# Delta-rule attention and routed experts: keys and queries times the states of two heads in one block-diagonal product, the masked product on four array positions, ranks in two products

## The chip, the cores and the metric

The kernel runs on one core of a Trainium2 chip. The metric is the device time of one execution in microseconds (us). A core has a matrix engine (PE, with its weight loads listed as PEld), a vector engine (DVE), a scalar engine (ACT), GpSimd (POOL) and a queue engine (SP). [...] Each engine runs its own instructions in order and waits for semaphores of the others.

## The reference

Attention with a delta rule on 4 x 8 heads, 768 steps, head dimension 48, and a top-1 mixture of 8 experts on the 3072 resulting rows of 384:

```python
for t in range(S):
    kt, vt, bt = (k_n[:, :, t], v[:, :, t], beta[:, :, t, None])
    y[:, :, t] = np.einsum('bhd,bhde->bhe', q[:, :, t], state)
    v_old = np.einsum('bhde,bhd->bhe', state, kt)
    state = state + bt[:, :, :, None] * np.einsum('bhd,bhe->bhde', kt, vt - v_old)
...
logits = x @ w_gate
expert_idx = np.argmax(logits, axis=1)
...
for e in range(E):
    lo, hi = (boundaries[e], boundaries[e + 1])
    h = np.maximum(x_sorted[lo:hi] @ w1[e], 0.0)
    y_sorted[lo:hi] = h @ w2[e]
return (gate_w[:, None] * y).astype(np.float32)
```

k_n is k over its norm, x the attention output with the heads side by side, gate_w the softmax weight of the chosen expert.

## The kernel before

All data are float32. The 768 steps are cut into 12 chunks t of 64 steps. The 32 heads are numbered by f (8), e (2) and x (2): e picks the half of the 128 partitions in which the 48 features of a head stand (partitions 64e to 64e+47), x the half in which its 64 steps stand. `products()` runs over the 32 heads. A float32 product is two passes, a pass being one weight load and one matmul, so a group of 32 products is 64 passes.

For each chunk, `scores(t)` (L311) multiplies keys with keys and queries; every two chunks `invert(n)` inverts triangular 32 x 32 blocks on DVE, with some 170 short instructions; `turn(t)` is the recurrence: `values` (L495) puts v into the PSUM banks BR, `with_state` (L480) adds keys times the state, ACT copies the sum to R, `inverse` (L512), `across` (L522) and `inverse` again give Z, with an ACT copy behind each, and `kz` (L536) adds keys times Z to the state in the banks BS, which ACT copies to S for the next chunk. `output(t)` is `with_state` again for the queries (into the banks BY) and `masked` (L557), 32 products of the masked scores with Z; ACT copies the rows x and SP writes them to `xs` in DRAM. Bank BR+e holds all heads of one e.

`logits(t)` transposes the rows (L578) and multiplies them with the gate (L586). `route(m, part)` works on groups of four tiles of 128 rows (five groups, then two groups of two): part 0 finds the expert on DVE (one-hot `oh`), part 1 ranks the rows within their experts by `ranks` on PE (L632, L638: for four tiles 8 products, 16 passes) and POOL writes (row, gate) entries into two lists in DRAM (L669, one indirect DMA per tile).

Expert 0 takes its first 256 rows early: `early_rows` loads their entries (`both_e`), a minimum of the two lists gives `rows_e` (L865), and POOL gathers the rows. `entries` loads the rest after the last route (`both_l`, three DMAs on SP and three on ACT; `rows`, L763). `turned_rows` (L797), `hidden` (L815) and `second` (L844, L897 for the last 32 rows) are the experts; `weights(e)` loads 3 MB on SP in five DMAs.

The order on each engine is not the order of the code. A planner (class `Plan`) takes every operation with its estimated cost, passes and priority, plays it forward and emits all engines in the order of the starts that it finds; `passes` feeds a model of the matrix engine's instruction pages (PAGE 128 passes, FILL 3.8).

## Time and profile before

| | |
|---|---|
| three runs | 646.66, 647.83, 650.55 us, median 647.83 |
| the profiled execution | 645.72 us, span 644.0 us, mean granted clock 0.875 |
| busy | PE 84%, PEld 58%, DVE 35%, ACT 23%, POOL 16% |
| 0 to 57 us | loads, first scores, first inversion |
| 57 to 310 us | chunks 0 to 11 and routing |
| 310 to 644 us | early rows of expert 0, then the experts |

The span counts from the first to the last instruction; 1.7 us of the execution lie around it. The granted clock is a share of TensorE's full speed; it has two levels, so a mean of 0.75 says that half of the stretch ran at each. A busy PE may still be waiting inside a group of passes.

### The profile page before, as it was taken

The page shows a single profiled execution, that of the slowest core. Times are in us where ns is not written, and L with a number is a line of the kernel's source. Part 1 is how long each engine was busy: PE and PEld are TensorE (multiplying, and loading weights), DVE is VectorE, ACT ScalarE, POOL GpSimd, SP SyncE. Part 2 cuts the span into 40 slices and gives each one's busy share as a digit, 9 for nine tenths or more (in the row PEclk, how much of TensorE's full clock was granted, in tenths as well). Part 3 has the DMA queues.
Part 4 walks back from the last instruction along what each step waited for, and adds up shares of the span by engine and source line. Part 5 has one row for each costly group of instructions (what it writes and reads, how often), then busy time and mean ns, then how long its engine had stood idle before and what let it go on. Part 6 is the DMA issues. An engine that isn't in the chain of part 4 may idle for free. (4 is left out here: it accounts for less than half of the span.)

```text
span 644.0 us, 17055 instructions
## 1 busy us (share of the span) xinstructions
PE 540.8 (84%) x7496; PEld 374.6 (58%) x7497; DVE 226.1 (35%) x921; ACT 151.2 (23%) x297; POOL 101.8 (16%) x109
## 2 busy tenths in 40 slices
PE   4448878989889978947696799999999999999990
PEld 4236667977777857746454555555555555555550
DVE  2976998885775680002100111201111101210100
ACT  2453445245244322321000110111101010110100
POOL 2000000320201002020206030402213040201011
PEclk9999879688588756755697899999999999999996
DMA  8964424433123225207403523433422340100000
GB/s 197 241 136 133 135 79 122 137 98 114 52 63 100 77 94 183 92 3 246 133 3 96 182 78 110 154 100 128 145 85 88 107 160 1 39 1 24 14 12 24
DMA packets 29933, 64.16 MB, mean 100 GB/s; under 512 B 6006, under 2 KB 18214, under 8 KB 29856
## 3 DMA queue, kind: packets, MB, share of 16 engines
q1 hardware_dynamic: 24240, 52.47, 27.0%
q0 software_dynamic: 4352, 9.47, 4.7%
q10 hardware_dynamic: 1264, 1.10, 0.8%
q8 instruction: 59, 0.97, 0.7%
q14 instruction: 18, 0.15, 0.1%
HBM read 49.62 MB, written 11.04 MB: 94 GB/s over the span
## 5 line engine op out<-in xcount | busy, mean ns | idle before, releaser
L815 PE MATMUL pair<-kqA,blkA 128*128 128x416 f32 (+2 forms) x288 | 91.7, 477 | 5.8 <-ACT kqA L824 4.3
L844 PE MATMUL pair<-blkA,kqA 128*128 128x384 f32 x240 | 80.0, 491 | 0.0
L815 PEld LDWEIGHTS pair<-kqA,blkA 128*128 128x128 f32 x288 | 55.2, 205 | 39.8 <-issue 28.6
L821 DVE TENSOR_SCALAR kqA<-pair 128x416 f32<-128x416 f32 (+2 forms) x36 | 19.5, 543 | 144.9 <-PE pair L815 83.1
L844 PEld LDWEIGHTS pair<-blkA,kqA 128*128 128x128 f32 x240 | 45.0, 190 | 34.7 <-issue 5.6
L744 POOL DMA_INDIRECT out<-y,rows_i x30 | 28.9, 963 | 224.3 <-ACT y L835 157.5
L311 PE MATMUL pair<-kqA 48*64 48x128 f32 (+1 forms) x896 | 38.7, 329 | 26.2 <-ACT pA L256 15.4
L815 PE MATMUL pair<-kqA,pA 128*128 128x416 f32 x144 | 51.1, 514 | 0.3 <-ACT y L835 0.3
L512 PE MATMUL pair<-R,blkA 32*32 32x48 f32 x1536 | 36.2, 253 | 17.4 <-issue 9.4
L311 PEld LDWEIGHTS pair<-kqA 48*64 48x64 f32 x896 | 31.3, 184 | 31.5 <-ACT pA L256 17.8
L844 PE MATMUL pair<-pA,kqA 128*128 128x384 f32 x144 | 48.1, 491 | 0.0
L824 ACT ACTIVATE kqA<-pair 128x416 f32<-128x416 f32 (+2 forms) x36 | 17.2, 478 | 131.2 <-PE pair L815 93.3
L669 POOL DMA_INDIRECT lists<-ent,ri x24 | 27.9, 1162 | 108.7 <-DVE ri L657 57.6
L512 PEld LDWEIGHTS pair<-R,blkA 32*32 32x32 f32 x1536 | 30.5, 154 | 22.9 <-issue 12.5
L832 DVE TENSOR_SCALAR y<-pair,rows 32x384 f32<-32x384 f32 (+1 forms) x15 | 8.5, 607 | 92.8 <-ACT y L835 85.4
L815 PEld LDWEIGHTS pair<-kqA,pA 128*128 128x128 f32 x144 | 27.1, 190 | 22.7 <-issue 21.1
L844 PEld LDWEIGHTS pair<-pA,kqA 128*128 128x128 f32 x144 | 26.9, 190 | 21.2 <-issue 3.7
L480 PE MATMUL pair<-S,kqA 48*64 48x48 f32 x1408 | 34.5, 250 | 3.0 <-issue 2.9
L835 ACT ACTIVATE y<-pair,rows 128x384 f32<-128x384 f32 x15 | 8.7, 580 | 113.9 <-PE pair L844 108.3
L737 POOL DMA_INDIRECT kqA<-xs,rows_i x30 | 29.8, 994 | 27.3 <-DVE rows_i L734 18.4
L480 PEld LDWEIGHTS pair<-S,kqA 48*64 48x64 f32 x1408 | 30.4, 163 | 5.7 <-issue 5.1
L557 PE MATMUL pair<-Z,pA 64*64 64x48 f32 x768 | 33.5, 258 | 0.0
(113 smaller groups left out, 677.9 us busy)
## 6 DMA issues: line engine op xcount, KB each, us to landing
kqA<-in_kq SPq DMA_DIRECT2D x46, 192.0 KB, 4.4
blkA<-in_w SPq DMA_DIRECT2D x15, 512.0 KB, 4.3
blkA<-in_w SPq DMA_DIRECT2D x10, 768.0 KB, 5.2
v<-in_vtok SPq DMA_DIRECT2D x12, 384.0 KB, 3.6
kt<-in_ktok SPq DMA_DIRECT2D x12, 384.0 KB, 6.1
xs<-x SPq DMA_DIRECT2D x24, 192.0 KB, 2.1
pA<-in_w SPq DMA_DIRECT2D x9, 512.0 KB, 4.7
pA<-in_w SPq DMA_DIRECT2D x6, 768.0 KB
```

The lines of the kernel that those rows point to most:

```text
L311: nc.tensor.matmul(bk[bank + e][half(x), i * w : i * w + w].rearrange("p (k c) -> p k c", c=C), lhsT=v[feat(e), 0, x * FQ + f, :], rhs=v[f ...
L480: nc.tensor.matmul(sh(bank + e)[half(x), f, :], lhsT=KQ(t)[feat(e), k, x * FQ + f, :], rhs=Sbs[t % 2][feat(e), x, f, :], start=first and f ...
L512: nc.tensor.matmul(sh(BZ + e)[quad(q), f, :], lhsT=tt[quad(q), :, 16 * u + 8 * e + f], rhs=R[quad(q), e, f, :], start=True, stop=True, ski ...
L557: nc.tensor.matmul(sh(BY + e)[half(x), f, :], lhsT=Pm(t)[half(x), e, f, :], rhs=Zbs[t % 2][half(x), e, f, :], start=(t == 0 and f == 0), s ...
L669: P.op("POOL", 1.0, lambda i=i: nc.gpsimd.indirect_dma_start(out=lists[i % 2], out_offset=bass.IndirectOffsetOnAxis(ap=ri[:, i : i + 1], a ...
L737: nc.gpsimd.indirect_dma_start(out=dst, out_offset=None, in_=xs, in_offset=bass.IndirectOffsetOnAxis(ap=idx, axis=0), bounds_check=N - 1, ...
L744: nc.gpsimd.indirect_dma_start(out=out, out_offset=bass.IndirectOffsetOnAxis(ap=idx, axis=0), in_=src, in_offset=None, bounds_check=N - 1, ...
L815: nc.tensor.matmul(bk[b][:, 0:n], lhsT=a1[:, s, f * 128 : f * 128 + 128], rhs=xT[:, s, :], start=(s == 0), stop=(s == NK - 1))
L821: (lambda f=f, b=b: nc.vector.tensor_scalar(out=hT[:, f, :], in0=bk[b][:, 0:n], scalar1=0.0, scalar2=None, op0=OP.max))
L824: (lambda f=f, b=b: nc.scalar.activation(out=hT[:, f, :], in_=bk[b][:, 0:n], func=AF.Relu)),
L835: (lambda: nc.scalar.activation(out=y[0:n], in_=bk[b][0:n, 0:DM], func=AF.Copy, scale=gate)),
L844: nc.tensor.matmul(bk[b][:, 0:DM], lhsT=hT[:, f, at : at + 128], rhs=a2[:, f, :], start=(f == 0), stop=(f == NF - 1))
```

## The change

- `with_state`: the states of two heads (e = 0 and 1) stand as diagonal blocks of a 128 x 96 tile, so that one product with 112 partitions and 96 columns serves both: 16 products (32 passes) in place of 32 (64 passes). The keys and queries need zeros in the partitions between the heads: POOL clears ring slots, one is cleared by DMA, and the state tiles are cleared once.
- BR, BZ and BY now hold bank by f // 4, with e inside; R, Z and v follow. Each masked product and each query product of f >= 4 writes the other half of the partitions, which the host turns back.
- The copy of the state is two: the half of the partitions with e = 0 on ACT, that with e = 1 on DVE.
- `ranks`: two products (4 passes) on all tiles at once; their second operand `up` is a running sum that DVE makes (a copy and n - 1 additions).
- `both_e` is loaded from POOL's queue, `both_l` from SP's alone, and the weights of experts 1 and 2 wait for `rows`.
- Costs and passes of the planner follow, and the order of all engines with them.

```diff
+    P.op("DVE", 1.0, lambda: nc.vector.memset(pairs[1][:], 0.0), w=kb(BR), prio=-49)
+    for i in range(2):
+        P.op("POOL", 1.4, lambda i=i: nc.gpsimd.memset(Sbs[i][:], 0.0), w=[("S", i, e) for e in range(2)], prio=-15)
+    for i in (2, 3, 4, 5):
+        P.op("POOL", 1.85, lambda i=i: nc.gpsimd.memset(kqA[:, 2048 * i : 2048 * i + 2048], 0.0),
+             w=kKQ(i) + [("zero", i)], prio=-60)
+    for e in range(2):
+        r = slice(64 * e + D, 64 * e + 64)
+        P.op("SP", 0.6, dma(nc.sync, kqA[r, 2048:4096], kqA[r, 10240:12288]), r=[("zero", 5)], w=[("zero", 1)],
+             prio=-40, lat=2.5)
...
     def with_state(t, bank, k, first):
-        for f, e, x in products():
-            nc.tensor.matmul(
-                sh(bank + e)[half(x), f, :], lhsT=KQ(t)[feat(e), k, x * FQ + f, :],
-                rhs=Sbs[t % 2][feat(e), x, f, :], start=first and f == 0, stop=True,
-                skip_group_check=True,
-            )
+        for i in range(4):
+            for g in range(2):
+                for x in range(2):
+                    f = 4 * g + i
+                    nc.tensor.matmul(
+                        bk[bank + g][half(x ^ g if first else x), 2 * D * i : 2 * D * i + 2 * D],
+                        lhsT=KQ(t)[0 : 64 + D, k, x * FQ + f, :], rhs=Sbs[t % 2][0 : 64 + D, x, f, :],
+                        start=first and i == 0, stop=True, skip_group_check=True,
+                    )
...
-            P.op("PE", 1.15, lambda: with_state(t, BR, 0, False), r=kKQ(t, (0,)) + [("S", t % 2)], w=kb(BR), prio=t, passes=64)
+            P.op("PE", 1.5, lambda: with_state(t, BR, 0, False), r=kKQ(t, (0,)) + kS(t), w=kb(BR), prio=t, passes=32)
...
-            P.op("ACT", 0.75, copy("ACT", both(Sbs[(t + 1) % 2]), two(BS)),
-                 r=kb(BS), w=[("S", (t + 1) % 2)], prio=-90)
+            for e in range(2):
+                q = "DVE" if e else "ACT"
+                P.op(q, 0.83, copy(
+                    q, Sbs[(t + 1) % 2][half(e), :, :, D * e : D * e + D],
+                    pairs[BS // 2][half(e), :, 0:DM].rearrange("p x (f d) -> p x f d", d=D)),
+                    r=kb(BS), w=[("S", (t + 1) % 2, e)], prio=-90)
...
         def masked():
-            for f, e, x in products():
-                nc.tensor.matmul(
-                    sh(BY + e)[half(x), f, :], lhsT=Pm(t)[half(x), e, f, :], rhs=Zbs[t % 2][half(x), e, f, :],
-                    start=(t == 0 and f == 0), stop=True, skip_group_check=True,
-                )
-        P.op("PE", 2.0, masked, r=[("P", t % RING), ("Z", t % 2)], w=kb(BY), prio=t + OUT, passes=64)
+            for i in range(4):
+                for e in range(2):
+                    for g in range(2):
+                        for x in range(2):
+                            f = 4 * g + i
+                            nc.tensor.matmul(
+                                at(BY, f, e)[half(x ^ g)], lhsT=Pm(t)[half(x), e, f, :],
+                                rhs=Zbs[t % 2][half(x), f, e, :],
+                                start=(t == 0 and i == 0 and e == 0), stop=True, skip_group_check=True,
+                            )
+        P.op("PE", 1.2, masked, r=[("P", t % RING), ("Z", t % 2)], w=kb(BY), prio=t + OUT, passes=64)
...
+            dve(32, lambda: nc.vector.tensor_copy(out=up[:, 0:n], in_=oh[:, 0:n]), [K("oh")], [K("up")], pr)
+            for i in range(1, n):
+                dve(8, lambda i=i: nc.vector.tensor_tensor(
+                    out=up[:, i], in0=up[:, i], in1=up[:, i - 1], op=OP.add), [], [K("up")], pr)
...
-            for i in range(n):
-                nc.tensor.matmul(
-                    ps[:, i * E : i * E + E], lhsT=const("upper"), rhs=oh[:, i, :],
...
-            for i in range(n):
-                k = n - i
...
+            nc.tensor.matmul(
+                ps[:, 0 : n * E], lhsT=const("upper"), rhs=oh[:, 0:n].rearrange("p n e -> p (n e)"),
+                start=True, stop=True, skip_group_check=True,
+            )
+            nc.tensor.matmul(
+                ps[:, E : n * E + E], lhsT=const("ones"), rhs=up[:, 0:n].rearrange("p n e -> p (n e)"),
+                start=False, stop=True, skip_group_check=True,
+            )
...
     def entries():
...
-            e, q = ((nc.sync, "SP"), (nc.scalar, "ACT"))[i]
+            e, q = nc.sync, "SP"
...
-            e, q = ((nc.sync, "SP"), (nc.scalar, "ACT"))[i]
-            P.op(q, 0.3, dma(e, both_e[:, i], lists[i][0 : EARLY * E].rearrange("(p t e) o -> p t e o", t=2, e=E)[:, :, 0, :]),
+            e, q = nc.gpsimd, "POOL"
+            P.op(q, 1.0, dma(e, both_e[:, i], lists[i][0 : EARLY * E].rearrange("(p t e) o -> p t e o", t=2, e=E)[:, :, 0, :]),
...
-    weights(1, 20)
-    weights(2, 21)
+    weights(1, 20, ["rows"])
+    weights(2, 21, ["rows"])
```

On PE, around the first route's ranks, the order before runs the query product of chunk 3 ahead of the logits and eight products of ranks between them and the next key product (L480 is `with_state`, pair_95 the banks BR, pair_97 BY, pair_96 BZ):

```order
L578 MATMUL pair_96<-cf,x_79 128x128 x3
L480 MATMUL pair_97<-S_73,kqA 64x48 x32
L586 MATMUL pair_96<-wg,xT_80 128x8 x3
L586 MATMUL pair_96<-wg,xT_81 128x8 x3
L632 MATMUL pair_96<-oh_128,cf 128x8 x4
L638 MATMUL pair_96<-oh_128,cf 128x32
L638 MATMUL pair_96<-oh_128,cf 128x24
L638 MATMUL pair_96<-oh_128,cf 128x16
L638 MATMUL pair_96<-oh_128,cf 128x8
L480 MATMUL pair_95<-S_72,kqA 64x48 x32
L557 MATMUL pair_97<-Z_76,pA 64x48 x32
L512 MATMUL pair_96<-R,blkA 32x48 x32
```

The changed kernel has two rows for the ranks (L668, L672), 16 products in each `with_state` (L502), and the masked product (L590) ahead of the logits (L618):

```order
L590 MATMUL pair_97<-Z_76,pA 64x48 x32
L618 MATMUL pair_96<-wg,xT_80 128x8 x3
L618 MATMUL pair_96<-wg,xT_81 128x8 x3
L668 MATMUL pair_96<-oh_128,cf 128x32
L672 MATMUL pair_96<-up_136,cf 128x32
L502 MATMUL pair_95<-S_72,kqA 64x96 x16
L323 MATMUL pair_97<-kqA 64x128 x16
L537 MATMUL pair_96<-R,blkA 32x48 x32
```

On POOL, from the fifth route's four list entries to the first gathers of the experts, the order before is (rows_ei are the early rows, rows_i the rest, L744 writes results):

```order
L669 DMA lists<-ent_140,ri_142 24832x2 x4
L669 DMA lists<-ent_141,ri_143 24832x2
L737 DMA kqA<-xs,rows_ei 128x384 x2
L669 DMA lists<-ent_141,ri_143 24832x2
L669 DMA lists<-ent_140,ri_142 24832x2 x2
L737 DMA kqA<-xs,rows_i 32x384
L744 DMA out<-y_108,rows_ei 3072x384
L737 DMA kqA<-xs,rows_i 128x384 x4
```

In the changed kernel the loads of both_e and the early gathers stand ahead of all entries of the last two routes, and the second gather of the late rows ahead of the first write of results:

```order
L702 DMA lists<-ent_142,ri_144 24832x2 x4
L244 DMA both_e<-lists 128x2x2 x2
L770 DMA kqA<-xs,rows_ei 128x384 x2
L702 DMA lists<-ent_143,ri_145 24832x2 x2
L702 DMA lists<-ent_142,ri_144 24832x2 x2
L770 DMA kqA<-xs,rows_i 32x384
L770 DMA kqA<-xs,rows_i 128x384 x2
L777 DMA out<-y_108,rows_ei 3072x384
```

On DVE, inside the inversion of the second pair of chunks, the changed kernel has the first copy of a state (rt, ra and b belong to the inversion, v is scaled for the chunks):

```order
L404 TENSOR_TENSOR rt_119<-rb_117,blkA 128x32
L259 COPY S_73<-pair_94 64x16x48
L406 TENSOR_SCALAR rt_119<-rt_119 128x32
L408 RECIPROCAL ra_115<-rt_119 128x32
L413 STREAM_TRANSPOSE nt_83<-rt_119 128x32
L409 TENSOR_TENSOR b_121<-ra_115,bl 128x32
```

Before, DVE had no work between `kz` and the next `with_state`; each of 11 state copies is now such a row in DVE's order.

## Rows read from the trace of the kernel before

**Rows 1.** The page: busy time by engine, and the instruction queue (packets, MB).

```profile
PE 540.8 (84%) x7496; PEld 374.6 (58%) x7497; DVE 226.1 (35%) x921; ACT 151.2 (23%) x297; POOL 101.8 (16%) x109
...
q8 instruction: 59, 0.97, 0.7%
```

**Rows 2.** Stretches of time: busy us by engine, granted clock, DMA share, GB/s.

```profile
57.00:231.00 174.00, 152.87 (x4550) 131.22 (x4549) 131.66 (x601) 73.24 (x133) 22.64 (x20) 0.80 0.36 105
231.00:310.00 79.00, 57.60 (x1245) 49.74 (x1246) 16.59 (x100) 18.77 (x40) 11.90 (x12) 0.59 0.37 124
...
62.90:72.68 9.78, 7.23 (x320) 6.11 (x320) 8.74 (x46) 5.45 (x8) 0.00 (x0) 1.00 0.53 144
205.60:212.00 6.40, 3.86 (x75) 2.50 (x70) 5.88 (x26) 0.31 (x2) 4.42 (x4) 0.50 0.04 5
276.30:282.10 5.80, 0.00 (x0) 0.00 (x0) 0.00 (x0) 0.81 (x1) 3.21 (x4) 0.50 0.02 1
```

**Rows 3.** Timeline of PE, chunk 8: start us, length us, line, passes.

```profile
200.49 1.15 PE L480 MATMUL pair<-S,kqA 48*64 48x48 f32 x64
...
203.76 1.96 PE L480 MATMUL pair<-S,kqA 48*64 48x48 f32 x64
...
211.77 3.65 PE L557 MATMUL pair<-Z,pA 64*64 64x48 f32 x64
...
217.85 1.14 PE L512 MATMUL pair<-R,blkA 32*32 32x48 f32 x64
...
222.07 2.07 PE L557 MATMUL pair<-Z,pA 64*64 64x48 f32 x64
```

**Rows 4.** Groups of PE instructions, 57 to 310 us: passes, busy us, mean ns, idle before.

```profile
L480 PE MATMUL pair<-S,kqA 48*64 48x48 f32 x1408 | 34.5, 250 | 3.0 <-issue 2.9
L557 PE MATMUL pair<-Z,pA 64*64 64x48 f32 x768 | 33.5, 258 | 0.0
...
L638 PE MATMUL pair<-oh,cf 128*128 128x16 f32 (+3 forms) x48 | 9.8, 345 | 0.0
L632 PE MATMUL pair<-oh,cf 128*128 128x8 f32 x48 | 8.4, 301 | 3.4 <-DVE fi L623 1.6 <-ACT xT L256 0.9 <-ACT lg L256 0.8
```

**Rows 5.** Timeline of PE in the expert stage, at clock 1.00.

```profile
329.22 10.48 PE L844 MATMUL pair<-blkA,kqA 128*128 128x384 f32 x32
...
360.61 1.50 PE L897 MATMUL pair<-blkA,kqA 128*32 128x384 f32 x16
```

**Rows 6.** Waits of PE, 57 to 283 us: us in total, times, longest.

```profile
PE pair L512 <- issue: 9.4, 12, 2.7
PE pair L522 <- ACT Z L256: 7.7, 3, 5.9
...
PE pair L480 <- issue: 2.9, 11, 0.4
```

**Rows 7.** ACT's state copy in the trace (min, median, max ns), and DVE's longest wait.

```profile
L256 ACT ACTIVATE S<-pair x11: 799/810/815, 60.1 to 264.9; 128x768 f32<-128x768 f32 x11
...
DVE pA L343 <- ACT pA L256: 21.0, 5, 8.1
```

**Rows 8.** Timeline, from the scan's last products to the late rows.

```profile
302.13 1.45 PE L586 MATMUL pair<-wg,xT 128*128 128x8 f32 x6 [0.65 <-ACT xT L256]
303.30 0.16 DVE L865 TENSOR_TENSOR rows_e<-both_e 128x4 f32<-128x4 f32 x1 [2.08 <-DMA both_e<-lists]
...
310.02 1.48 PE L797 MATMUL pair<-cf,kqA 128*128 128x128 f32 x4 [2.97 <-DMA kqA<-xs,rows_ei]
...
325.31 0.33 ACTq L243 DMA_DIRECT2D both_l<-lists  x1
...
330.18 0.22 DVE L763 TENSOR_TENSOR rows<-both_l 128x66 f32<-128x66 f32 x1
...
341.91 1.04 POOL L737 DMA_INDIRECT kqA<-xs,rows_i  x1 [0.31 <-issue]
...
345.07 1.12 PE L797 MATMUL pair<-cf,kqA 128*128 128x128 f32 x4 [5.36 <-DMA kqA<-xs,rows_i]
```

More of the change, by code (lines that the diff above doesn't have):

```diff
@@ L193, in tile_kernel @@
     kts = [pool.tile([128, 2 * FQ, D], FP32, name=f"kt{i}") for i in range(2)]
-    vs = [pool.tile([128, 2 * FQ, D], FP32, name=f"v{i}") for i in range(2)]
-    Sbs = [pool.tile([128, 2, FQ, D], FP32, name=f"S{i}") for i in range(2)]
-    R = pool.tile([128, 2, FQ, D], FP32, name="R")
-    Zbs = [pool.tile([128, 2, FQ, D], FP32, name=f"Z{i}") for i in range(2)]
+    vs = [pool.tile([128, FQ, 2, D], FP32, name=f"v{i}") for i in range(2)]
+    Sbs = [pool.tile([128, 2, FQ, 2 * D], FP32, name=f"S{i}") for i in range(2)]
+    R = pool.tile([128, FQ, 2, D], FP32, name="R")
+    Zbs = [pool.tile([128, FQ, 2, D], FP32, name=f"Z{i}") for i in range(2)]
     xbs = [pool.tile([128, DM], FP32, name=f"x{i}") for i in range(3)]
@@ L475, in both, with kS @@
     def both(a):
[L476 removed]
+        return a[:].rearrange("p (g f) e d -> p g (f e d)", g=2)
     def with_state(t, bank, k, first):
[L479 to L484 removed]
+        for i in range(4):
[7 more added lines that the diff above has]
+                    )
+    def kS(t):
+        return [("S", t % 2, e) for e in range(2)] + [("zero", t % RING)]
     def turn(t):
@@ L537, in kz @@
                         sh(BS + x)[feat(e), f, :], lhsT=kt[half(x), e * FQ + f, :],
-                        rhs=Z[half(x), e, f, :], start=(t == 0 and f == 0), stop=True,
+                        rhs=Z[half(x), f, e, :], start=(t == 0 and f == 0), stop=True,
                         skip_group_check=True,
@@ L630, in ranks @@
             ps = bk[BZ]
-            for i in range(n):
-                nc.tensor.matmul(
-                    ps[:, i * E : i * E + E], lhsT=const("upper"), rhs=oh[:, i, :],
-                    start=(i == 0), stop=(i == 0), skip_group_check=True,
-                )
-            for i in range(n):
-                k = n - i
-                nc.tensor.matmul(
-                    ps[:, (i + 1) * E : (n + 1) * E].rearrange("p (k e) -> p k e", e=E),
-                    lhsT=const("ones"), rhs=oh[:, i : i + 1, :].to_broadcast([128, k, E]),
-                    start=False, stop=True, skip_group_check=True,
-                )
-        P.op("PE", 0.5 * n, ranks, r=[K("oh"), "cf"], w=[("bk", BZ)], prio=pr, passes=4 * n)
+            nc.tensor.matmul(
[6 more added lines that the diff above has]
+            )
+        P.op("PE", 0.5, ranks, r=[K("oh"), K("up"), "cf"], w=[("bk", BZ)], prio=pr, passes=4)
         dve(40, lambda: nc.vector.tensor_tensor(
@@ L680, in wview, with weights @@
         )
-    def weights(e, pr):
+    def weights(e, pr, behind=()):
         i = e % 3
@@ L695, in weights @@
                  dma(nc.sync, a1[:, s, :], w1[e].rearrange("(s p) f -> p s f", p=128)[:, s, :]),
-                 w=[("w", i, s)] + extra, prio=pr + s)
+                 r=behind, w=[("w", i, s)] + extra, prio=pr + s)
         for h in range(2):
@@ L700, in weights @@
                      w2[e].rearrange("(c p) d -> p c d", p=128)[:, 4 * h : 4 * h + 4, :]),
-                 w=[("w", i, 3 + h)] + extra, prio=pr + 3 + h)
+                 r=behind, w=[("w", i, 3 + h)] + extra, prio=pr + 3 + h)
     LAST = 3 * E
@@ L947, in tile_kernel @@
                 invert(i // 2)
+            if i == 2:
+                P.op("POOL", 1.85, lambda: nc.gpsimd.memset(kqA[:, 0:2048], 0.0), w=kKQ(0) + [("zero", 0)], prio=0)
     entries()
     early()
-    weights(1, 20)
-    weights(2, 21)
+    weights(1, 20, ["rows"])
+    weights(2, 21, ["rows"])
     fetch(0)
@@ L1066 @@
     r = _run(nc, [arrays], core_ids=[0])
-    got = r.results[0]["out_0"]
-    return np.ascontiguousarray(
-        got.reshape(NT, 2, 2, C, DM).transpose(2, 1, 0, 3, 4).reshape(N, DM)
-    )
+    got = r.results[0]["out_0"].reshape(NT, 2, 2, C, DM).copy()
+    got[:, 1] = got[:, 1, ::-1]
+    return np.ascontiguousarray(got.transpose(2, 1, 0, 3, 4).reshape(N, DM))
```

43 lines of the change are left out of this document (22 added, 21 removed).

## The prediction, on record before the result

> **What bounds the kernel now.** I read the stretches of time first, then PE's timeline, its groups, the waits, and last the places where one stage hands over to the next. From 57 to 231 us PE is busy 152.9 of 174.0 us and DVE 131.7, so PE sets the pace there and DVE has 42.3 us to spare; from 231 to 310 us, with the inversions over, DVE has little left to do and the chain of chunks 9 to 11 runs through PE and ACT [rows 2]. From 345 us on the experts keep PE nearly full; the change leaves their products as they are, so all that it can do lies ahead of that.
>
> PE's pace has two sources. One is the clock: the same 64 passes of `with_state` took 1.15 us at 200.49 and 1.96 us at 203.76, the masked product 2.07 us at 222.07 and 3.65 us at 211.77 [rows 3]. These are the two levels; a mean of 0.80 from 57 to 231 us is a share of 0.6 at full clock, 0.59 from 231 to 310 us a share of 0.18 [rows 2]. The other is the supply of instructions. The page has 59 packets on the instruction queue, and PE ran 7496 + 7497 instructions, 254 to a packet, that is 127 passes [rows 1]. In the stretch from 62.90 to 72.68 us at full clock PE got through 320 passes in 9.78 us, 30.6 ns each, though it was busy only 7.23 us [rows 2]; the list of its waits names "issue", a wait for nothing that the profile shows, as the releaser ahead of L512 and L480 [rows 6]. At two places it is worse: 75 passes in 6.40 us while POOL wrote list entries, and none in 5.80 us from 276.30 us [rows 2], which is also the 5.9 us ahead of L522 [rows 6]. I take these for pages of PE's code that came late. That is an inference: no row shows a page arriving.
>
> **The change part by part**, against the profiled execution, 645.7 us.
>
> *Masked product: -15 us.* It has 12 groups of 64 passes, 33.5 us in all [rows 4]; with 2.07 and 3.65 us that is 6.5 groups at full clock and 5.5 at half. Before, only two array positions took part (x to x). The query product of the same size, 64 rows, 64 columns of weights, 48 columns, used all four and took 1.15 and 1.96 us [rows 3]. At these, 12 groups take 18.3 us. The ends are 0 (no second pair at once) and -15; I take the row of the same shape.
>
> *Keys and queries times states: +15 us on PE.* 22 groups took 34.5 us [rows 4], which fits 11 at 1.15 and 11 at 1.96 us. A new product spans both row halves, so only two column halves work at once, and it has 96 columns where there were 48. No row has this shape. The nearest is the product for the last 32 rows, full rows on four column positions: 16 passes of 384 columns in 1.50 us [rows 5], 94 ns a pass; 96 columns on two positions cost 94 x 4/2 x 96/384 = 47 ns, so 32 passes take 1.5 us at full clock and 3.0 at half. 11 x 1.5 + 11 x 3.0 = 49.5 us against 34.5. Below, if the columns cost nothing and only the number of passes counts, it is half, -17 us; above, if the column halves do not overlap, 99 us, +64. I take the middle, since that row has both full rows and column positions.
>
> *Ranks: -12 us.* 96 passes took 9.8 + 8.4 = 18.2 us [rows 4], 0.19 us each; seven groups of 4 passes are 5.3 us. DVE's additional copies and sums (four instructions in each of five routes, two in each of two, at some 0.2 us, an estimate from the 0.16 us of L865 [rows 8]) stand ahead of ranks; PE waited 3.4 us ahead of L632 in all, so at those places they add about 1 us.
>
> *Supply of instructions: -14 us.* 704 passes go with `with_state` and 68 with ranks, 772 of 7496. At 30.6 ns that is 23.6 us, the most it can give; where PE is held by the clock or by longer passes it gives nothing. PE's "issue" waits (9.4 + 2.9 for two of the lines) with the 5.9 us ahead of L522 [rows 6] and the slow 6.40 us, which at the 17.8 ns a pass of L512's group at 217.85 us [rows 3] would have been 1.3 us, come to some 21 us (half of the last is in the first). I take two thirds of these, 60% of the other, since the new group after the ranks holds half the passes and lasts longer, so that a page has more time to come.
>
> Here the Trainium skill speaks against the change: "Runtime: NRT & Kernel Launch", section "Instruction fetch mechanics", says that code comes in blocks of 16 KiB and that crossing a block is mostly hidden. The packets agree with the block (0.97 MB over 59 is 16.4 KB); the waits in rows 2 and 6 do not look hidden. By that rule this term is 0 and the sum 625 us.
>
> *State copies on DVE: 0.* ACT's copy of 128 partitions took 0.81 us [rows 7]; half the partitions have the same 768 columns, so ACT's part stays at 0.81 and DVE gets 11 of about 0.83, 9 us, plus the 24 short ones, some 5 us. DVE's 42.3 idle us cover that, and they also limit what the stretch to 231 us can gain to about 28 us. Its longest wait, 21.0 us, is for ACT's score copies [rows 7], which follow PE, so it usually arrives early. The new wait is DVE's for `kz`; behind it queue the inversion's steps. If each of 11 waits cost 2 us to the next key product, +22.
>
> *Clearing and start: 0.* POOL's memsets and DVE's additional one run while the first loads are awaited, and the first state is needed only after the first inversion. The loads of slots 2 to 5 now wait for the memsets, and SP's queue behind them; the scores of those chunks are due later. If the cover failed I would put it at 2 us.
>
> *Early rows: -5.5 us.* `rows_e` waited for `both_e` until 303.30 and PE, whose last logits ended at 303.58, began the experts at 310.02 [rows 8]. Now POOL issues the loads right after the fifth route's entries, which it wrote around 276.30 us [rows 2], over 20 us before. The transposes can follow the logits at once, except for the last ranks: 6.4 less 0.9.
>
> *Late rows: -5.4 us.* The last `both_l` load left ACT's queue only at 325.31 us, behind evictions, so `rows` came at 330.18, and the gather that PE needed stood behind a write of results and left at 341.91; PE idled 5.36 us until 345.07 [rows 8]. On SP all six leave one behind the other after the last entry, and that gather stands ahead of the write. The weights of experts 1 and 2 move behind `rows`; they have the early part, from 310.02 us to the end of L844's group at 339.70 [rows 5, 8], to land, and SP has nothing else queued behind them that is due.
>
> Sum: -15 + 15 - 12 - 14 - 5.5 - 5.4 = -36.9, so 608.8 us for an execution like the profiled one. The median of the runs lies 2.1 us above that one: **611 us**.
>
> **The rivals.**
> - *PE's waits are not a matter of code, 625 us.* They come with POOL's entry writes in any case, or pages are hidden. For it: both worst places have POOL busy (4.42 and 3.21 us) [rows 2]. Against: 30.6 ns a pass with POOL idle [rows 2].
> - *The masked product stays at its time, 626 us,* if two row halves cannot write one bank at once: x = 0 and 1 of one f share bank BY + g. Against it: L512 has 64 passes of 48 columns in 1.14 us [rows 3], 17.8 ns each; a pass of 384 columns takes 327 ns [rows 5], so 48 columns 41 ns, and 2.3 passes ran at once, though L512 uses two banks and each bank gets two row ranges. One per bank would allow 2.0. The Trainium skill, "TensorEngine Tiling (Array Packing)", "Gotcha 1: PSUM Pressure", states just that different row tiles cannot access the same PSUM bank simultaneously; the trace disagrees by a small margin.
> - *The clock stays up, 598 us.* Between the groups at 200.49 and 203.76 us PE had only ranks, 8 to 32 columns wide, for 2.1 us, and the second of the two ran at half clock [rows 3]. If the share at full clock from 231 to 310 us rose from 0.18 to 0.6, 57.6 busy us [rows 2] would become 57.6 x 1.4/1.82 = 44.3, -13.
> - *Slower, 660 us:* the column halves do not overlap in the full-row shape, +64 in place of +15. It decides from 87 us for the 22 groups, 3.9 us each, against 2.25 assumed. Against it is L897's overlap of four.
> - *DVE's copies are late, 633 us,* by the price above. For it: DVE's order is set by the planner's guess of PE's times.
>
> **How the numbers follow.** The forecast 0.53; no code relief 0.17; clock 0.13; masked 0.07; DVE 0.06; slower 0.04. The range 594 to 634 us takes in the forecast with its bounds (supply between 0 and -23.6, hand-overs 3 us either way) and the first three and the last of the rivals. A measurement of this kernel can tell about 1% from no change; 641.4 us is that line, and only several rivals together or the slower one reach it: faster 0.92, same 0.04, slower 0.04.
>
> **What would show it.** In the changed trace a masked group should read about 1.15 or 1.96 us, a `with_state` group of 32 passes 1.5 or 3.0, ranks about 0.8; fewer "issue" waits on PE from 57 to 283 us; no wait of several us ahead of the experts' transposes; DVE's idle time shrunk to below 25 us by 231 us of the old count. The prediction is wrong if `with_state` reads over 4 us, if the scan's end moves by under 15 us, or if new PE waits name DVE's state copy.

## The result, and the profile after

The changed kernel took 617.25 us (median of four runs, 614.27 to 620.35) against 647.25 for the kernel before: ratio 0.9576, 95% interval 0.9472 to 0.968. The forecast was 611 us with a range of 594 to 634. Two later sets of runs gave 0.9627 (0.9589 to 0.9665) and 0.9574 (0.9521 to 0.9628). The profiled execution took 616.37 us, 29.4 less than the one before.

The page of the changed kernel, busy time by engine and the instruction queue (packets, MB), against [rows 1]:

```profile
PE 516.0 (84%) x6724; PEld 348.6 (57%) x6725; DVE 241.7 (39%) x957; ACT 151.2 (25%) x297; POOL 111.7 (18%) x118
...
q8 instruction: 53, 0.87, 0.6%
```

772 passes and 6 packets of code are gone. Groups of PE instructions of the changed kernel, 40 to 300 us (line, passes, busy us, mean ns, idle before), against [rows 4]:

```profile
L502 PE MATMUL pair<-S,kqA 112*64 112x96 f32 x704 | 35.3, 259 | 2.8 <-ACT pA L257 1.8 <-DVE S L259 1.1
...
L590 PE MATMUL pair<-Z,pA 64*64 64x48 f32 x768 | 16.8, 235 | 0.8 <-issue 0.8
...
L672 PE MATMUL pair<-up,cf 128*128 128x32 f32 (+1 forms) x14 | 3.1, 305 | 0.0
```

The masked product (L590) went from 33.5 to 16.8 us, the ranks from 18.2 to 3.1 + 3.1 (L668, not shown, has the same), `with_state` (L502) from 34.5 to 35.3. PE's timeline of the changed kernel, chunks 1 and 2, against [rows 3] (start us, length us; in brackets the idle time before and what ended it):

```profile
80.28 1.54 PE L502 MATMUL pair<-S,kqA 112*64 112x96 f32 x32
81.75 1.15 PE L590 MATMUL pair<-Z,pA 64*64 64x48 f32 x64
...
89.96 2.83 PE L502 MATMUL pair<-S,kqA 112*64 112x96 f32 x32 [1.60 <-ACT pA L257]
95.09 1.51 PE L537 MATMUL pair<-R,blkA 32*32 32x48 f32 x64 [2.31 <-DVE blkA L458]
```

A group of the new product takes 1.54 us at full clock and 2.83 at half, as assumed; a masked group 1.15. The last row is new: PE stands 2.31 us for the inversion (L458). What delays it is in the waits of DVE in the changed kernel, 57 to 284 us (us in total, times, longest), against [rows 7], where DVE's longest was for scores:

```profile
DVE S L259 <- ACT S L257: 38.8, 7, 14.4
```

Most of these 38.8 us is the wait for `kz` itself. But DVE's half of the state copy starts only when ACT's half has ended, and DVE's inversion steps queue behind it. The first state copy in the timelines of ACT and DVE of the changed kernel (60.13 + 0.80 is 60.93):

```profile
60.13 0.80 ACT L257 ACTIVATE S<-pair 64x768 f32<-64x768 f32 x1 [3.53 <-PE pair L561]
60.97 0.96 DVE L259 COPY S<-pair 64x768 f32<-64x768 f32 x1 [6.60 <-ACT S L257]
```

The hand-over of the changed kernel, against [rows 8]:

```profile
282.54 1.45 PE L618 MATMUL pair<-wg,xT 128*128 128x8 f32 x6 [0.58 <-ACT xT L257]
283.84 1.09 PE L830 MATMUL pair<-cf,kqA 128*128 128x128 f32 x4
...
304.56 10.48 PE L877 MATMUL pair<-blkA,kqA 128*128 128x384 f32 x32
...
314.88 0.60 PE L830 MATMUL pair<-cf,kqA 128*128 128x128 f32 x4
```

The experts follow the last logits at once (the modelled end of one row lies 0.15 us past the start of the next), and the late rows follow the early part at once. The 29.4 us, stage by stage (the end of the logits is their start plus their length, 283.99 in the changed kernel):

| stage | before | after | difference |
|---|---|---|---|
| to the end of the last logits | 303.58 | 283.99 | -19.6 |
| from there to the experts' first transposes | 6.44 | -0.15 | -6.6 |
| from there to the late rows' transposes | 35.05 | 31.04 | -4.0 |
| from there to the end of the span | 298.9 | 299.7 | +0.8 |

The hand-overs came about as forecast. The scan was to gain 26 us and gained 19.6 here; in the profiles of the two later sets the changed kernel's logits end at 288.77 and 288.43 us, about 15 before the 303.58 of the kernel before, which was not profiled in those sets. The experiments ask where the rest went.

### The profile page after: what moved, and what is told of

Its sections match the earlier page's. It is cut to its first block, busy times and chain, and to the rows that moved or that the text cites. A ratio compares the mean times of both kernels' runs of the same rounds, so it can differ in the third digit from the quotient of the medians.

```text
span 614.6 us, 15547 instructions
## 1 busy us (share of the span) xinstructions
PE 516.0 (84%) x6724; PEld 348.6 (57%) x6725; DVE 241.7 (39%) x957; ACT 151.2 (25%) x297; POOL 111.7 (18%) x118
## 5 line engine op out<-in xcount | busy, mean ns | idle before, releaser
L877 PE MATMUL pair<-blkA,kqA 128*128 128x384 f32 x240 | 80.0, 491 | 0.0
L854 DVE TENSOR_SCALAR kqA<-pair 128x416 f32<-128x416 f32 (+2 forms) x36 | 19.6, 544 | 140.8 <-PE pair L848 85.6
L323 PE MATMUL pair<-kqA 48*64 48x128 f32 (+1 forms) x896 | 40.5, 329 | 31.8 <-ACT pA L257 17.2
L877 PEld LDWEIGHTS pair<-blkA,kqA 128*128 128x128 f32 x240 | 45.0, 190 | 34.7 <-issue 5.6
L537 PE MATMUL pair<-R,blkA 32*32 32x48 f32 x1536 | 34.4, 241 | 16.8 <-ACT R L257 8.2
L877 PE MATMUL pair<-pA,kqA 128*128 128x384 f32 x144 | 48.1, 491 | 0.0
L537 PEld LDWEIGHTS pair<-R,blkA 32*32 32x32 f32 x1536 | 29.2, 150 | 22.2 <-ACT R L257 10.1
L848 PEld LDWEIGHTS pair<-kqA,pA 128*128 128x128 f32 x144 | 27.1, 190 | 22.7 <-issue 21.1
L877 PEld LDWEIGHTS pair<-pA,kqA 128*128 128x128 f32 x144 | 26.9, 190 | 21.2 <-issue 3.8
L502 PE MATMUL pair<-S,kqA 112*64 112x96 f32 x704 | 35.3, 259 | 2.8 <-ACT pA L257 1.8
L702 POOL DMA_INDIRECT lists<-ent,ri x24 | 24.9, 1038 | 63.2 <-DVE ri L690 27.4
L502 PEld LDWEIGHTS pair<-S,kqA 112*64 112x64 f32 x704 | 32.0, 145 | 4.5 <-ACT pA L257 2.4
L257 ACT ACTIVATE blkA<-pair 128x512 f32<-128x512 f32 x22 | 23.3, 1057 | 26.3 <-PE pair L323 24.0
```

Source lines behind the costliest of these rows:

```text
L257: return lambda: nc.scalar.activation(out=o, in_=i, func=AF.Copy, scale=scale)
L323: nc.tensor.matmul(bk[bank + e][half(x), i * w : i * w + w].rearrange("p (k c) -> p k c", c=C), lhsT=v[feat(e), 0, x * FQ + f, :], rhs=v[f ...
L502: nc.tensor.matmul(bk[bank + g][half(x ^ g if first else x), 2 * D * i : 2 * D * i + 2 * D], lhsT=KQ(t)[0 : 64 + D, k, x * FQ + f, :], rhs ...
L537: nc.tensor.matmul(at(BZ, f, e)[quad(q)], lhsT=tt[quad(q), :, 16 * u + 8 * e + f], rhs=R[quad(q), f, e, :], start=True, stop=True, skip_gr ...
L702: P.op("POOL", 1.0, lambda i=i: nc.gpsimd.indirect_dma_start(out=lists[i % 2], out_offset=bass.IndirectOffsetOnAxis(ap=ri[:, i : i + 1], a ...
L848: nc.tensor.matmul(bk[b][:, 0:n], lhsT=a1[:, s, f * 128 : f * 128 + 128], rhs=xT[:, s, :], start=(s == 0), stop=(s == NK - 1))
```

## The experiments

The kernel before took 623.8 us on the chip of the first set, 641.8 in the second set and 644.7 in the third, so kernels are compared within a set, or by their ratio to the kernel before. The expectations of the first set speak of 617 us, the time of the first measurement; for its four kernels the ratio is what counts. The theory: the change gains as predicted by passes, ranks, hand-overs and less code, and DVE's copies take some back. Rivals: the masked product's time is hidden; the slow supply of instructions comes from POOL's list writes and not from the amount of code.

**First set, one part undone in each.**

*e1_state_act*: both halves of the state are copied by ACT. The planner then also puts some of PE's groups in another order, from the first chunk on.

```diff
-                q = "DVE" if e else "ACT"
+                q = "ACT"
```

> Both halves of the state copy on ACT, two copies one behind the other; all else as in the changed kernel (617 us). Theory A (DVE's 38.8 us of waits for the state copies delay the inversions, chunk 2's first inverse product came at 95 us where it was 87 before): without these waits the first inverse product of chunk 2 comes at about 88 us, the last logits some 6 us earlier, total about 610 us (606 to 614). Theory B (DVE waited where it had slack): 617 us within 3. Theory C (ACT's chain gets longer by 0.8 us in each of 11 chunks): up to 626 us.

Ratio 0.960 (0.9511 to 0.9688). This does not differ from the changed kernel's in the other sets; it was run again beside it (below). PE's first inverse product of chunk 2 came at 91.22 us without the wait for L458, where 88 was expected, and the last logits end at 267.88 us, 0.95 before those of e4_queues_old of the same set, where 6 were expected.

*e2_masked_two*: the masked product on two array positions, in the same order of instructions on PE; the host no longer turns the rows back.

```diff
-                        bk[bank + g][half(x ^ g if first else x), 2 * D * i : 2 * D * i + 2 * D],
+                        bk[bank + g][half(x), 2 * D * i : 2 * D * i + 2 * D],
...
-                                at(BY, f, e)[half(x ^ g)], lhsT=Pm(t)[half(x), e, f, :],
+                                at(BY, f, e)[half(x)], lhsT=Pm(t)[half(x), e, f, :],
```

> The masked product back on two array positions, with the same order of instructions; all else as in the changed kernel. Each masked group should read 2.07 us at full clock or 3.65 at half again (1.15 and 1.96 on four). Theory A (the masked product lies on PE's path, 16.8 us in the changed kernel's groups against 33.5 before): 631 us (626 to 636). Theory B (another engine or the instruction supply sets the pace in much of the scan): 617 to 623 us. If two row halves could not write a bank at once, the groups would not change at all.

Ratio 0.9648 (0.9566 to 0.9729), only 0.2 to 0.7% above the changed kernel's three ratios, 1 to 5 us and inside the intervals (the changed kernel itself was not run in this set), though PE's masked groups have their old length back. From the groups of PE, 40 to 300 us, of this kernel:

```profile
L502 PE MATMUL pair<-S,kqA 112*64 112x96 f32 x704 | 35.4, 260 | 2.3 <-ACT pA L257 2.2
...
L590 PE MATMUL pair<-Z,pA 64*64 64x48 f32 x768 | 27.7, 231 | 0.0
L323 PE MATMUL pair<-kqA 48*64 48x128 f32 x511 | 22.6, 321 | 6.6 <-ACT pA L257 5.5 <-issue 1.0
L520 PE MATMUL pair<-v,cf 128*128 128x384 f32 x44 | 22.3, 640 | 0.0
```

Beside it stands e4_queues_old of the same set, whose order on PE is that of the changed kernel up to the eleventh `kz`. The same view of it:

```profile
L502 PE MATMUL pair<-S,kqA 112*64 112x96 f32 x704 | 37.4, 268 | 2.9 <-ACT pA L257 1.8 <-DVE S L259 1.0
...
L520 PE MATMUL pair<-v,cf 128*128 128x384 f32 x44 | 24.6, 699 | 0.0
...
L590 PE MATMUL pair<-Z,pA 64*64 64x48 f32 x768 | 15.7, 234 | 0.2 <-issue 0.2
```

From the first `kz` to the eleventh the two took 181.4 and 181.3 us. Of 12 us more in the masked product 4.3 us came back in L502 and L520, whose work is the same and of which more ran at full clock (granted clock of that stretch 0.88 against 0.85), and 4.2 us in shorter waits (PE was idle for 22.2 us of it against 26.4).

*e3_ranks_eight*: the ranks again in eight products for four tiles.

```diff
-                ps[:, 0 : n * E], lhsT=const("upper"), rhs=oh[:, 0:n].rearrange("p n e -> p (n e)"),
+            for i in range(n):
+                    ps[:, i * E : i * E + E], lhsT=const("upper"), rhs=oh[:, i, :],
...
+            for i in range(n):
+                    lhsT=const("ones"), rhs=oh[:, i : i + 1, :].to_broadcast([128, k, E]),
```

> Ranks back in eight products (16 passes for four tiles), DVE's running sums left in, same order; all else as in the changed kernel. Theory A (PE's path alone): 12 us more, 629 us, the granted clock of the scan as it is. Theory B (the narrow ranks let the clock fall, so that the groups behind them run at half clock): more than that, 635 to 640 us, and the with_state groups behind the ranks read 2.8 us and not 1.5, the clock from 220 to 260 us of the count falls from 0.88 to 0.65. Theory C (hidden under other waits): under 622 us.

Ratio 0.9803 (0.9706 to 0.9899), 1.8 to 2.3% above the changed kernel's, 11 to 14 us; beside e1 of the same set it is 13.6 us more (612.02 and 598.44). The term of -12 us is met: these products are 16.9 us here, 6.5 in e4, and about the whole difference is in the kernel's time. The granted clock of the late scan did not fall: 0.81 from the eighth `kz` to the last logits, 0.82 in e4. Groups of PE of this kernel, 40 to 300 us:

```profile
L675 PE MATMUL pair<-oh,cf 128*128 128x16 f32 (+3 forms) x48 | 9.3, 331 | 0.0
L669 PE MATMUL pair<-oh,cf 128*128 128x8 f32 x48 | 7.6, 283 | 1.1 <-ACT lg L257 1.1
```

*e4_queues_old*: the loads of list entries on their old queues, and the weights no longer behind `rows`.

```diff
-            e, q = nc.sync, "SP"
+            e, q = ((nc.sync, "SP"), (nc.scalar, "ACT"))[i]
...
-            e, q = nc.gpsimd, "POOL"
+            e, q = ((nc.sync, "SP"), (nc.scalar, "ACT"))[i]
...
-    weights(1, 20, ["rows"])
+    weights(1, 20)
```

> Loads of both_e and both_l back on SP's and ACT's queues, and the weights of experts 1 and 2 no longer waiting for rows; all else as in the changed kernel. Theory A (the two hand-overs gave 6.6 and 5.5 us): PE waits some 3 us for the early gathers and 5 us for the late ones again, total 628 us (624 to 631). Theory B (the early gain came from the planner's other order and the shorter tail, not from the queues): 620 to 624 us.

Ratio 0.9749 (0.9655 to 0.9842), 1.2 to 1.7% above, 8 to 11 us (its interval just touches that of a0_after_again below), and the two waits of [rows 8] are back in PE's timeline:

```profile
274.25 0.90 PE L830 MATMUL pair<-cf,kqA 128*128 128x128 f32 x3 [5.11 <-DMA kqA<-xs,rows_ei]
...
310.22 1.11 PE L830 MATMUL pair<-cf,kqA 128*128 128x128 f32 x4 [6.64 <-DMA kqA<-xs,rows_i]
```

**Second set: the changed kernel again, the products apart, the supply.**

*a0_after_again*: the changed kernel.

> The changed kernel once more, unchanged, so that the other kernels of this set stand beside it on one chip. The kernel before took 647.3 us on one chip and 623.8 us on another, so the ratio is what can be carried over. If the gain is a share of the scan's work: ratio 0.95 to 0.965 again, and the products of keys and queries with the states again at about 35 us between 40 and 300 us. If the gain came only because the first chip granted less clock to the kernel before (0.58 late in its scan): ratio above 0.97 where the kernel before is near 624 us.

616.92 us, ratio 0.9627 (0.9589 to 0.9665). The gain is there in another set too.

*e7_old_products*: the kernel before, with the changed kernel's ranks and queues; what is missing are the block-diagonal states, the new banks, the state copy in two halves and the masked product on four positions. Its edit to the kernel before is the hunks of the change on `ranks`, `up`, `weights` and the entry loads, as above.

```diff
+            dve(32, lambda: nc.vector.tensor_copy(out=up[:, 0:n], in_=oh[:, 0:n]), [K("oh")], [K("up")], pr)
...
+                ps[:, 0 : n * E], lhsT=const("upper"), rhs=oh[:, 0:n].rearrange("p n e -> p (n e)"),
...
+    weights(1, 20, ["rows"])
```

> The kernel before with the ranks in two products and with the four moved transfers of the changed kernel, but with the old products: one head's state a product on four positions, the masked product on two. If ranks and hand-overs carry their terms (12 + 11 us) and the new products carry 15 + 0 and lose some of it to VectorE's waits: 0.965, between the kernel before and the changed one, and the products on the states show 25 to 28 us where the kernel before had 34.5, since the clock is no longer low behind the ranks. If the saving of 704 products on the states also saves instruction supply of 14 us: 0.98 or above.

619.38 us, ratio 0.9682 (0.9631 to 0.9733): ranks and hand-overs give 22.4 us of the 24.9 that the whole change gave beside it (641.79, 619.38 and 616.92 us). The products give the remaining 2.5 us, which the intervals do not tell from nothing. Groups of PE, 40 to 300 us, of this kernel:

```profile
L557 PE MATMUL pair<-Z,pA 64*64 64x48 f32 x768 | 32.6, 251 | 0.1
L480 PE MATMUL pair<-S,kqA 48*64 48x48 f32 x1408 | 29.2, 237 | 1.1 <-issue 0.9 <-ACT pA L256 0.2
```

The same view of a0_after_again:

```profile
L502 PE MATMUL pair<-S,kqA 112*64 112x96 f32 x704 | 39.8, 279 | 2.8 <-ACT pA L257 1.8 <-DVE S L259 1.0
...
L590 PE MATMUL pair<-Z,pA 64*64 64x48 f32 x768 | 16.4, 235 | 0.4 <-issue 0.3
```

The old product on the states costs 29.2 us here, not 34.5, and the new one 39.8: +10.6, against -16.2 of the masked product. PE's two lines get 5.6 us shorter, of which 2.5 arrive, within the noise.

*e5_state_64*: each product on the states is cut in two with the same weights, 704 passes more, the same columns.

```diff
-                        bk[bank + g][half(x ^ g if first else x), 2 * D * i : 2 * D * i + 2 * D],
+                    for e in range(2):
+                            at(bank, f, e)[half(x ^ g if first else x)],
...
+                            rhs=Sbs[t % 2][0 : 64 + D, x, f, D * e : D * e + D],
```

> Each of the 32 products of a group on the states is cut into two products of 48 columns with the same weights, so a group has 64 again and the same columns go through; 704 matmuls and 704 weight loads more. If a group's time goes by columns alone: 1.54 us a group and no change beyond 1%. If it goes by the number of products: 64 at four positions took 1.15 us and these stand at two, so up to 2.3 us a group at full clock, 0.8 x 22 = +17 us on TensorE and about +2.7% in all. If the supply of instructions is what counts: groups near 1.54 us, but TensorE's waits for issue grow by up to 14 us and the kernel by up to 2.2%.

632.86 us, ratio 0.9842 (0.9768 to 0.9917), 15.9 us above a0. From PE's timeline of this kernel:

```profile
81.42 2.11 PE L503 MATMUL pair<-S,kqA 112*64 112x48 f32 x64
```

A group takes 2.11 us and not 1.54, 66 ns for the two passes that run at once, where 96 columns take 96 ns. The old form, 48 rows on four positions, took 1.15. The masked product shows the same with its shape unchanged: 64 passes of 48 columns took 2.07 us on two positions and 1.15 on four. So a pass of 48 columns held its position for some 65 ns, more than half of what 96 columns took, and the block-diagonal form is longer than the one it replaced because it gives up two of four positions. 22 groups at 0.57 us more are 12.5 of the 15.9 us; the number of passes counts by PE's time, and little is left for the amount of code: PE's "issue" waits from 57 us to the last logits are 12.4 us with these 704 passes more and 10.2 in a0.

*e6_no_entries*: the list writes of the first five routes are left out, so the early tokens' experts find empty lists and the output lacks their part.

```diff
-        for i, t in enumerate(g):
+        for i, t in enumerate(g if m > 4 else ()):
             P.op("POOL", 1.0, lambda i=i: nc.gpsimd.indirect_dma_start(
```

> Leaves out the twenty writes of list entries by GpSimd's indirect transfers for the first five routings, so the experts of the early tokens find empty lists and the output of those tokens lacks its expert part. In the changed kernel's trace TensorE's products came slowly one after another in the stretches where these writes were issued (128.8 to 137, 167 to 174, 203 to 210, 241 to 246 and 261 to 266 us). If the writes are the cause: these drips vanish, TensorE's issue waits of 40 to 300 us fall from 17 us to below 5, the scan ends 10 to 20 us sooner and the kernel is 2 to 3% faster than the changed one. If the drips come with the entry to new code or from transfers of any kind: they stay where they were and the kernel is within 1%. What the experts do is of the same size with empty lists, except for the gathered rows themselves.

591.43 us, ratio 0.9219 (0.9154 to 0.9284): 25.5 us (4.1%) less than a0, where 2 to 3% were expected, and more than any part of the change. PE's order is the same up to the eleventh `kz`; from the first to the eleventh it took 178.9 us, where the three profiles of the changed kernel have 193.1, 198.1 and 197.4. The rest of the 25.5 us lies behind, and part of it may come from what no longer has to wait for the lists: the experts' second product (L877) starts 7.3 us after the last logits and not 21.1, while PE then waits 14.7 us for the late rows' gather.

**Third set: what it is in the list writes.**

*a1_after_third*: the changed kernel.

> The changed kernel unchanged, to stand beside the next three on one chip: 0.955 to 0.965 of the kernel before, as on the two chips so far (0.9576 and 0.9627).

617.37 us, ratio 0.9574 (0.9521 to 0.9628), as expected.

*e8_entries_skipped*: the list writes of the first five routes are issued, but a bound lets only index 0 through, so nearly nothing reaches the lists and the output lacks the same part; the order of instructions is the changed kernel's.

```diff
-                in_=ent[:, i, :], in_offset=None, bounds_check=E * NL - 1, oob_is_err=False),
+                in_=ent[:, i, :], in_offset=None, bounds_check=E * NL - 1 if m > 4 else 0, oob_is_err=False),
```

> The twenty list writes of the first five routings are still issued by GpSimd, in the same order of instructions on every engine, but their bound lets only index 0 through, so hardly an entry is moved and those tokens lack their expert part. If it is the moved entries (small packets on the queues that also bring instructions) that slow TensorE: as without the writes, 0.92 of the kernel before and no drips. If it is GpSimd's own work of making the descriptors, or the order of instructions that the kernel without writes also changed: the drips stay and the ratio stays at 0.95 to 0.965.

Ratio 0.9526 (0.9459 to 0.9592): the gain of e6 is not there. Timeline of POOL in this kernel, the second route:

```profile
168.22 0.98 POOL L702 DMA_INDIRECT lists<-ent,ri  x1 [2.72 <-DVE rb L398]
169.50 1.38 POOL L702 DMA_INDIRECT lists<-ent,ri  x1 [0.30 <-issue]
171.19 0.97 POOL L702 DMA_INDIRECT lists<-ent,ri  x1 [0.30 <-issue]
172.47 0.98 POOL L702 DMA_INDIRECT lists<-ent,ri  x1 [0.30 <-issue]
```

And of PE in the same kernel at the same time:

```profile
169.55 0.32 PE L537 MATMUL pair<-R,blkA 32*32 32x48 f32 x4 [0.43 <-issue]
170.32 0.32 PE L537 MATMUL pair<-R,blkA 32*32 32x48 f32 x4 [0.44 <-issue]
171.09 0.38 PE L537 MATMUL pair<-R,blkA 32*32 32x48 f32 x4 [0.45 <-issue]
171.82 0.39 PE L537 MATMUL pair<-R,blkA 32*32 32x48 f32 x3 [0.35 <-issue]
```

While POOL works on its writes PE gets three or four passes every 0.75 us, where a group of 64 otherwise takes 1.13. The kernel before has the same in the second route, with its entries moved:

```profile
163.38 0.47 PE L480 MATMUL pair<-S,kqA 48*64 48x48 f32 x3 [0.35 <-issue]
164.15 0.47 PE L480 MATMUL pair<-S,kqA 48*64 48x48 f32 x4 [0.30 <-issue]
```

In e6, without writes, the same L537 of that chunk is one row:

```profile
162.37 1.13 PE L537 MATMUL pair<-R,blkA 32*32 32x48 f32 x64
```

So PE is held back where POOL issues an indirect write, whether or not its entries reach the lists. The writes' packets were not taken away by this, though. Their queue on the pages of a1_after_third, e8 and e6, in this order (packets, MB, most of it gathered rows):

```profile
q0 software_dynamic: 4416, 9.47, 4.9%
...
q0 software_dynamic: 4416, 1.62, 1.1%
...
q0 software_dynamic: 3776, 1.61, 1.1%
```

Without the 20 writes 640 packets are missing, 32 for each; with the bound they are all there. POOL's own work and these packets are therefore not told apart. The expectation puts these packets on the queues that bring instructions; the pages list instructions on q8 and q14.

The slow rows also depend on the chip. The kernels of the first set issue the same writes, and there PE runs on in nearly whole groups: beside the 20 writes it has 1 to 4 "issue" waits in each of these four profiles, and 8 to 20 in the eight others with the writes. Timeline of POOL and of PE in e4_queues_old, the second route:

```profile
162.23 0.97 POOL L702 DMA_INDIRECT lists<-ent,ri  x1 [2.73 <-DVE rb L398]
163.51 1.39 POOL L702 DMA_INDIRECT lists<-ent,ri  x1 [0.30 <-issue]
165.20 0.97 POOL L702 DMA_INDIRECT lists<-ent,ri  x1 [0.30 <-issue]
...
162.87 1.51 PE L537 MATMUL pair<-R,blkA 32*32 32x48 f32 x64
164.31 1.10 PE L323 MATMUL pair<-kqA 48*64 48x128 f32 x32
165.42 1.13 PE L547 MATMUL pair<-Z,blkA 32*32 32x48 f32 x64
```

From the first to the eleventh `kz` e4 took 181.3 us with its writes, hardly more than e6 without them on another chip. e1_state_act and e1b_state_act are one kernel on the first and the third set's chips: 180.6 and 194.8 us for that stretch, 5.2 and 9.2 us of "issue" waits, and 598.44 and 614.68 us in all. So most of what the first set's chip is faster by lies in this stretch; that it is all due to the writes is not shown.

*e9_before_no_entries*: the edit of e6 in the kernel before.

> The kernel before without the same twenty list writes (output lacks the same part). If the stretches of slow supply in the kernel before were these writes too, and not the amount of code: 0.955 to 0.965 of the kernel before, about 25 us less, as the changed kernel gained by it. If in the kernel before they were the amount of code (59 instruction packets against 53): above 0.98.

605.37 us, ratio 0.9385 (0.9329 to 0.9441), 39 us less, where 25 were expected. From the first to the eleventh `kz` it took 193.5 us in place of 204.8 (the latter in the first measurement). So the writes cost about 11 us of this stretch before the change, and 14 to 19 after it: the change left them as they were. Most of the rest lies at the hand-over, where the early rows no longer wait for lists and the experts' first products run ahead of the last logits: from the end of the logits to L844 it took 6.5 us, where [rows 5, 8] give 25.6. PE's "issue" waits from 57 us to the end of the scan's logits, summed over lines, are 15.6 us before and 10.8 after; without the writes they are 7.0 and 4.7.

*e1b_state_act*: e1_state_act again, beside the changed kernel.

> Both halves of the state copied by ScalarE again, now beside the changed kernel on one chip. In the changed kernel VectorE stands 6.35 and 2.81 us behind its first two state copies, with the triangular solve queued behind them, and TensorE waits 2.2 us for that solve at 94.9 us; with ScalarE that solve ran some 7 us sooner and the wait was gone. If the waits count: 2 to 4 us (0.3 to 0.6%) faster than the changed kernel. If ScalarE's second copy (0.8 us, eleven times, on the path to the next product on the states) costs the same: no difference; if it costs more: up to 9 us slower, ratio 0.975.

614.68 us, ratio 0.9535 (0.9492 to 0.9578), 2.7 us below a1_after_third: what the waits were priced at, but the intervals overlap, and in the profiles the last logits end only 1.1 us sooner (287.33 and 288.43). The mechanism is in the timeline of DVE in a0_after_again:

```profile
60.74 0.96 DVE L259 COPY S<-pair 64x768 f32<-64x768 f32 x1 [6.35 <-ACT S L257]
```

and of PE in e1b, where the row that answers to 95.09 above waits for nothing:

```profile
90.64 1.51 PE L537 MATMUL pair<-R,blkA 32*32 32x48 f32 x64
```

## Why the prediction was nearly right

The direction and the range held; the forecast was 6 us too low. That it came so near is in part luck: the term for the supply of instructions was some 10 us too large, the masked product gave 1 to 5 us in place of 15, the products on the states cost less than 15, and the last two errors cancelled. The sum of -36.9 us stands against 30.0, 24.9 and 27.3 measured in the three sets. By its own steps:

- *Masked product, -15:* right on PE (-16.7, and -16.2 beside e7). But PE's time was taken for the kernel's time, and e2 gets only 1 to 5 us from it.
- *Keys and queries times states, +15:* the price of a group was right (1.54 and 2.83 against 1.5 and 3.0). The half of the groups taken to run at half clock was too many: 35.3 us in the first profile, 39.8 and 39.0 in the later ones, against 49.5 assumed. The old product, beside e7, would have been 29.2. By these sums about 1 of 22 groups ran at half clock in the first profile, and 4 to 5 in the later ones. The two product terms were to cancel, and within 2.5 us they did, though neither stood at its size.
- *Ranks, -12:* shown by e3, 11 to 14 us.
- *Supply of instructions, -14:* **this is the step that failed.** "I take these for pages of PE's code that came late" took what comes with POOL's list writes for code. The writes account for more than half of the "issue" waits, and the change keeps all of the writes. With them the waits fell by 15.6 - 10.8 = 4.8 us; without them the change saves 7.0 - 4.7 = 2.3 us, and this is about what less code is worth (e5's 704 passes more cost 12.4 - 10.2 = 2.2). The term also counted the 5.9 us ahead of L522, which [rows 6] put down to ACT's copy of Z: the same wait, ahead of `across` beside the fifth route's writes, is still 4.08 us in the changed kernel (L547 at 264.79) and 0.92 in e6. The first rival had said it ("They come with POOL's entry writes in any case") with 0.17; its 625 us was 8 us too high, as the forecast was 6 too low. On blocks of code the Trainium skill, "Runtime: NRT & Kernel Launch", section "Instruction fetch mechanics", says that crossing one is mostly hidden. With the writes gone the trace agrees better than I allowed: 4.7 us of waits in some 200, though single ones of 1.0 us remain, and no row shows whether these are such crossings.
- *State copies on DVE, 0 (up to 22):* a little too kind. DVE's 11 copies of 0.96 us are covered, but they stand behind ACT's halves; e1b puts the cost at 2.7 us, 1.1 by its profile, without settling it. One of the signs of being wrong did come, in small: PE waits once, 1.05 us at 61.98 in the changed kernel, for DVE's state copy. Another is open: the scan's end moved by 19.6 us in the profiled pair, and by 14.8 and 15.2 in the later sets' profiles against the same profile before.
- *Masked stays at its time:* the rival is out. 64 passes from two row halves into one bank per f took 1.15 us, as long as the query product on four positions; at some 65 ns a pass (e5) that is more than three at once. The rule of "TensorEngine Tiling (Array Packing)" in the Trainium skill, section "Gotcha 1: PSUM Pressure", that different row tiles cannot access the same PSUM bank simultaneously, does not show in that time.
- *The clock stays up, -13:* it did in part, and the forecast did not count on it. From the eighth `kz` to the last logits the granted clock was 0.64 before and 0.80, 0.80 and 0.74 in the three profiles of the changed kernel. The ranks were not what lowered it where this could be seen (e3). What the rise gave was not taken apart. The rival's own sum is a little off: with shares of time it is 57.6 x 0.59/0.80 = 42.5 us, -15.
- *Early and late rows, -5.5 and -5.4:* -6.6 and, after the wait that returns between the late transposes, -4.0 + 0.8. The waits that e4 brings back show it.

Summed from runs on several chips, for the profiled pair: ranks 12, hand-overs 9.8, products and copies 2.5 make 24.3 of 29.4 us. The other 5 us are no more than one profile differs from another (193.1 to 198.1 us for the same stretch of the changed kernel). Why the products' 5.6 us on PE arrive only in part was not taken apart further; e2 shows shorter waits and more full clock as the two ways by which such time is lost.

The best of the runs that compute the whole reference is e1b (0.9535), not told apart from the changed kernel.

## What to carry to other kernels

Look at what another engine does in the very stretch where instructions come slowly, before putting the wait down to the amount of code: a run that leaves that work out decides it, and a run that issues it without effect says how much of it counts. Do this on the chip that shows the wait: here one of the chips did not. Time saved on a busy engine is not time saved on the kernel; here a part was returned as clock and as waits, so undo each part alone. Short serial products on the path, such as the ranks, and transfers behind the wrong queue gave back about their whole length here, nine tenths of the gain of a change that was mostly about something else.

## What the runs showed of the hardware

- While POOL issued indirect writes, PE got three or four passes every 0.75 us, for some 5 us with four writes, whether or not the entries reached the lists (e8), and not without the writes (e6). Sixteen writes went with 11 to 19 us of the scan. On the chip of the first set the same writes left PE's groups nearly whole (e1 to e4). Through what the two are coupled, POOL's work or the packets, and why one chip is spared, was not found.
- A pass of 48 columns held its array position for about 65 ns (64 passes on two positions in 2.11 us), one of 96 columns for 96 ns, and on four positions 64 passes of 48 columns took 1.15 us. Halving the passes at twice the columns cost time here (1.54 against 1.15 us), since it gave up two positions.
- The same kernel before took 623.8 us on one chip and 641.8 to 647.8 in the other measurements; e1's kernel took 598.44 us on the former and 614.68 on one of the latter, 14.2 us of the difference between its profiles lying between the first and the eleventh `kz`.
